# A transformer block in one kernel: the differences of w_down one section later and on GpSimd alone, x in pieces at block changes, the sums of a block split between GpSimd and VectorE

## The chip, the cores and the metric

The kernel runs on one core of one Trainium2 chip. The metric is device time in microseconds (us) of one execution; every comparison is made against the kernel before, run on the same chip. The engines are named as in the profile: PE (TensorE, matmuls; PEld is its weight load), ACT (ScalarE), DVE (VectorE), POOL (GpSimd) and SP (SyncE, which here does little but issue DMAs, in the order of its program).

## The reference

```python
def _A_ref(x, wqkv, wo):                 # 32 heads of 18
    qkv = (x @ wqkv).reshape(B, S, 3, H, Dh).transpose(2, 0, 3, 1, 4)
    q, k, v = qkv[0], qkv[1], qkv[2]
    p = softmax(einsum("bhqd,bhkd->bhqk", q, k) * (Dh ** -0.5), axis=-1)
    o = einsum("bhqk,bhkd->bhqd", p, v)
    return o.transpose(0, 2, 1, 3).reshape(B, S, D) @ wo

def _B_ref(x, w_gate, w_up, w_down):
    return (gelu(x @ w_gate) * (x @ w_up)) @ w_down

xn = layernorm(x)                        # x: 1 x 2048 x 576, fp32
out = x + _A_ref(xn, wqkv, wo) * silu(_B_ref(xn, w_gate, w_up, w_down))   # w_gate, w_up: 576 x 4608; w_down: 4608 x 576
```

## The kernel before, in words

All matmuls keep fp32 accuracy by splitting each operand into a high and a low part of a shorter type and adding three products (high·high, low·high, high·low). So every weight that comes from memory is cut in two on its way: `split` (L116 to L121) makes the high part with a `tensor_scalar` on POOL (L118) and the low part with a `tensor_tensor` on POOL (L120); `split_ap` (L123) makes the high part on ACT instead.

The feed-forward part sets the frame. The 2048 tokens are four blocks of 512 (`TB`). For each block the 4608 hidden columns are done in 18 rounds of two sections (`g` = 0 and 1); a section is one slice of 128 columns, so there are 144 sections, numbered `n`. A section does 27 pairs of matmuls `pg` and `pu` (gate and up, L534) in three chunks of 9. While it runs, the weights of the next section are asked for (`load_gu`, L132, the tile `raw`) and are cut in three pieces `wh`/`wl` (`split_gu`), one after each chunk. Then the hidden values are activated and cut into `ah`/`al`.

Sections 10 to 137 (`ATT`) also carry the attention in between the matmuls: score matmuls `pe` (L1027) that ACT turns into exponentials `pT` (L1028), and matmuls `pm` (L974) whose maxima DVE takes (L977). At the end of each section with `g` = 1 stand 64 matmuls with the values, `acc` (L1062), which ACT and DVE carry into `accs`. Sections 0 to 9 are a lead without it.

The down projection of a round follows one round later. In block 0 it is the plain product (`half_downs`, L602, 96 matmuls `py`). From round 18 on it is a scheme with seven products of half-sized matrices (`seven_downs`, L672), which needs sums and differences of the four quarters of w_down. These are made once, in block 0, by `cut_down`: it cuts the raw w_down of the round into `bh`/`bl` for block 0's own product, makes four differences of quarters in place in `raw` (POOL, L719), takes their high part into `TY` (ACT, L721) and their low part back into `raw` (POOL, L722), and stores quarters and differences with six DMAs into `ds[r]` (L724 to L726). Blocks 1 to 3 read `bh`/`bl` back from there (`load_seven`). The first five raw w_down sit in tiles of the attention (`pT`), the others in `raw`.

`raw` has two buffers for gate/up loads and w_down loads alike (`raw_wide`). The PE program is fixed by hand. The other engines' programs are ordered by a scheduler, save where an instruction is held in the order of the code (`kept`, `pin`). Each DMA on SP waits for its data or its buffer before the next one in SP's program is issued.

At a block change the transposed x of the next block is loaded by `load_xd`: six DMAs (`xd`, L155), each with a copy of the upper half of the partitions into the lower, three copies on POOL (L161) and three on ACT (L159). In the last round of a block, `add_copied` (L698, two additions) and `combine` (L704, seven additions and subtractions over `Y`) put the block's seven sums together, all on DVE, and `store_y` writes them. The change from block 0 to 1 has no combine, since block 0's down product is plain.

Of the kernel before, what the change touches and what calls it, by code (L numbers as in the profile page):

```python
# [17 lines left out]
P = 128  # L18
NT = S // P
TB = 512  # L20
# [59 lines left out]
def kernel(ctx: ExitStack, tc: tile.TileContext, x, wqkv, wo, w_gate, w_up, w_down, out):  # L80
# [67 lines left out]

    def load_xd(b, apart=False):

        xd, copies = [[], []], [[], []]
        for c in range(0, NC, XG):
            for i in range(2):
                t = wts.tile([P, XG, TB], F32R, name=f"xd{i}_{c}")
                asked[:] = [nc.sync.dma_start(f(t)[0:HR], xhs[b][i, c * HR:(c + XG) * HR, :]  # L155
                                              .rearrange("(k p) t -> p k t", p=HR))]
                xd[i].append(t)
                if apart and i:
                    copies[i].append(lambda t=t: nc.scalar.activation(t[HR:P], t[0:HR], AF.Copy))  # L159
                elif apart:  # L160
                    copies[i].append(lambda t=t: nc.gpsimd.tensor_copy(t[HR:P], t[0:HR]))  # L161
                else:
                    nc.gpsimd.tensor_copy(t[HR:P], t[0:HR])
        return (xd, copies) if apart else xd


# [3 lines left out]
    with tc.tile_pool(name="pro", bufs=1) as pro, tc.tile_pool(name="pps", bufs=1, space=PSUM) as pps:  # L170
# [286 lines left out]
        for b in range(NB):  # L457
# [37 lines left out]
    FF = {"w": ahead, "xd": XD, "down": [], "n": 0, "keep": None, "late": [], "marks": False, "between": [], "added": None,  # L495
          "after": []}
    AH, AL = (ffn.tile([P, 7, HALF], F32R, name=m) for m in ("ah", "al"))
# [165 lines left out]
    def seven_downs(b, r):  # L663
# [4 lines left out]
        for n, (p, t) in enumerate(SUMS):  # L668
# [13 lines left out]
            if done in (3, 4) and FF["between"]:  # L682
                keep(FF["between"].pop(0)())
        if not fresh:
            FF["after"].append(add_copied)
        if r == NR - 1 or b * NR + r == SEVEN.stop - 1:
            FF["after"].append(lambda: combine(b, r))

    def add_copied():

        places = [(SUMS[n][1], PRODUCTS[SUMS[n][0]][2]) for n in COPIED]
        for t in range(2):
            at_t = [i for i, (tt, _) in enumerate(places) if tt == t]
            for i in at_t:
                assert places[i][1] == places[at_t[0]][1] + at_t.index(i)
            yy = Y[:, t, places[at_t[0]][1]:places[at_t[-1]][1] + 1, :]
            low = TY[:, at_t[0]:at_t[-1] + 1:2, :]
            keep(nc.vector.tensor_tensor(yy, yy, low, op=ALU.add))  # L698

    def combine(b, r):  # L700

        for to, x, y, op in ((C11, C11, Q1, ALU.add), (Q1, Q1, Q6, ALU.add), (C22, C22, Q1, ALU.add), (C21, C22, C21, ALU.subtract),
                             (C22, C22, Q5, ALU.add), (Q1, Q1, Q5, ALU.add), (C12, C12, Q1, ALU.add)):
            keep(nc.vector.tensor_tensor(Y[:, :, to, :], Y[:, :, x, :], Y[:, :, y, :], op=op))  # L704
        if r == NR - 1:
            store_y(b, range(TB // P))

# [4 lines left out]

    def cut_down(r, raw, wd, keep=lambda i: i):

        raw = raw.rearrange("p g (c n) -> p (g c) n", c=2)
        b11, b12, b21, b22 = range(4)
        split(wd[0].rearrange("p g (c n) -> p (g c) n", c=2), wd[1].rearrange("p g (c n) -> p (g c) n", c=2), raw, keep)
        for to, x, y in ((b11, b12, b11), (b12, b22, b12), (b22, b22, b11), (b21, b22, b21)):
            keep(nc.gpsimd.tensor_tensor(raw[:, to], raw[:, x], raw[:, y], op=ALU.subtract))  # L719
        high, low = TY.bitcast(F32R), raw.bitcast(F32R)  # L720
        nc.scalar.activation(high, raw, AF.Copy)  # L721
        keep(nc.gpsimd.tensor_tensor(low, raw, f(high), op=ALU.subtract))  # L722
        for i, (four, t) in enumerate(((BH, high), (BL, low))):
# [50 lines left out]
    def section(specials=(), tag="f", raw_d=None, ahead=True):  # L774
# [16 lines left out]
        if n + 1 < NF:  # L791
            nxt = load_gu((n + 1) % (NR * G), keep) if ahead else FF.pop("next_gu")
        if g == G - 1 and seven(n):
            load_seven(r)
        elif g == G - 1:
            FF["rawd"] = FF.pop("first_d") if n < G else load_down(
                r, raw_d() if raw_d else raw_wide().rearrange("p (g n) -> p g n", g=G)) if ahead else FF.pop("next_d")

        def splits(k):
            if nxt and ahead:  # L800
                first = split_gu(nxt, k, pin)
                if k == 0 and n in ATT and n > ATT.start and not seven(n):
                    no_sync(first, FF["hl"], "hidden values first")

        for k in range(NG - 1):
# [5 lines left out]
        FF["w"] = nxt  # L811
        copies = [[], []]
        if n + 1 < NF and (n + 1) % (NR * G) == 0:
            FF["xd"], copies = load_xd(b + 1, True)
            for m in copies[0]:
                pin(m())
        FF["act"], FF["rest"] = activate(pg, pu, n < ATT.stop, pin, seven(n) and g == 0)
        now = FF["down"] and FF["down"][0][-1] < FF["n"]
        if n < ATT.stop and not now:
            run_rest()  # L820
        for m in copies[1]:
            pin(m())
        if g == G - 1:
# [13 lines left out]
    def finish(pool=ffn, cut=split):  # L837
# [12 lines left out]
        if n % G == G - 1:  # L850
            wd = [pool.tile([P, G, D], F32R, name=m) for m in ("dh", "dl")] if pool is not ffn and (n // G) % 2 else \
                [down_pair(BH), down_pair(BL)]
            if b == 0:
                cut_down(r, FF["rawd"], wd)
            else:
                cut(*wd, FF["rawd"])
            for h in range(2):
# [492 lines left out]
```

## Time and profile before

| what | value |
|---|---|
| median of 3 runs (2846.18, 2846.45, 3736.32) | 2846.45 us |
| the profiled execution's own time | 2844.66 us |
| its span, first to last instruction | 2842.9 us |
| PE busy | 2582.8 us (91%) |
| DVE busy | 2084.6 us (73%) |
| POOL busy | 1692.8 us (60%) |
| ACT busy | 1603.0 us (56%) |
| mean granted TensorE clock | 0.949 |

The third of the three runs lies far from the other two, so the median is the upper of two that agree. Busy shares are means over stages that differ: block 0 lasts until 1034 us, blocks 1 and 2 have their changes near 1600 and 2200 us, and the rest is the end. In the rows of a chain the columns are start (us), duration (us), engine, tile and line, with "x64" for so many in a row; "DMA raw<-in_B_w_down_dram" is a transfer from w_down into `raw`. In the rows of a table of windows they are the stretch, its length, then for each engine the busy time and the number of instructions, the granted clock, the DMA share and GB/s.

### The profile page before, as it was taken

How to read it: one execution, taken by the hardware profiler on the slowest of the kernel's cores; microseconds unless marked ns; L12 is line 12 of the kernel's file. 1: busy time of each engine (PE TensorE's matmuls, PEld its weight loads, DVE VectorE, ACT ScalarE, POOL GpSimd, SP SyncE). 2: the span in 40 equal slices, each digit the busy share in tenths (PEclk: the TensorE clock that was granted, in tenths of full speed). 3: DMA queues.
4: the chain of work that ended last, by engine and by line, in shares of the span. 5: the costliest groups of instructions: out<-in, count | busy, mean ns of one | idle time of the engine just before them, and what ended most of it. 6: DMA issues, size and time to landing. Idle time of an engine off the chain costs nothing.

```text
span 2842.9 us, 59879 instructions
## 1 busy us (share of the span) xinstructions
PE 2582.8 (91%) x21496; PEld 1957.3 (69%) x21496; DVE 2084.6 (73%) x3650; ACT 1603.0 (56%) x3022; POOL 1692.8 (60%) x2043
## 2 busy tenths in 40 slices
PE   9974477779778799999999899999999899999999
PEld 8863466566565577777776667677777577767788
DVE  5311356567566678899999789899999789989477
ACT  3211125556455476677676667667677567767622
POOL 3113355554555566776666666676676567677775
PEclk9996778889898899999999999999999899999999
DMA  8865345545556577676666766666666666666584
GB/s 258 271 221 168 138 159 152 158 138 148 148 150 162 148 191 201 180 184 176 184 187 177 190 184 179 176 173 180 180 187 192 165 180 194 182 182 176 151 219 142
DMA packets 438743, 506.96 MB, mean 178 GB/s; under 512 B 116096, under 2 KB 312736, under 8 KB 438160
## 3 DMA queue, kind: packets, MB, share of 16 engines
q1 hardware_dynamic: 438064, 488.97, 61.1%
q10 hardware_dynamic: 384, 14.16, 1.2%
q8 instruction: 173, 2.83, 0.4%
q14 instruction: 122, 1.00, 0.1%
HBM read 411.13 MB, written 106.02 MB: 182 GB/s over the span
## 4 chain that ended last, share of the span: by engine, by line
PE 78%; DMA 9%; POOL 5%; DVE 3%; issue 2%; ACT 2%; SPq 1%; ACTq 0%; POOLq 0%; DVEq 0%
PE pg L534 26%; PE acc L1062 15%; PE py L672 10%; PE pe L1027 8%; PE pm L974 8%; PE po L196 5%; PE py L602 3%; PE pu L534 2%; PE po L1210 2%; DMA raw<-in_B_w_up_dram 2%; POOL bl L120 1%; POOL raw L719 1%; DMA xd<-xhs 1%; DMA raw<-in_B_w_down_dram 1%; DVE mx L977 1%
## 5 line engine op out<-in xcount | busy, mean ns | idle before, releaser
L977 DVE TENSOR_REDUCE mx<-pm 128x1 f32<-128x512 f32 x2048 | 1267.7, 682 | 286.5 <-PE pm L974 268.1
L1028 ACT ACTIVATE pT<-pe 128x512 f32<-128x512 f32 x2048 | 1151.8, 598 | 453.8 <-PE pm L974 315.0
L534 PE MATMUL pg<-xd,wh 64*128 64x512 f32 x2592 | 956.2, 402 | 0.0
L534 PE MATMUL pu<-xd,wh 64*128 64x512 f32 x2592 | 955.8, 402 | 0.1
L1027 PE MATMUL pe<-q,Ks 64*128 64x512 f32 x2048 | 797.1, 397 | 115.6 <-ACT pT L1028 114.8
L974 PE MATMUL pm<-Km,q 64*128 64x512 f32 x2048 | 806.7, 399 | 31.5 <-ACT accs L1065 16.9
L534 PEld LDWEIGHTS pg<-xd,wh 64*128 64x128 f32 x2592 | 493.3, 190 | 142.8 <-POOL ah L118 37.7
L120 POOL TENSOR_TENSOR wl<-raw,wh 128x384 fp32r<-128x384 f32 x432 | 438.6, 1016 | 249.9 <-PE pu L534 223.2
L534 PE MATMUL pg<-xd,wl 64*128 64x512 f32 x1296 | 512.3, 395 | 14.0 <-POOL wl L120 14.0
L534 PE MATMUL pu<-xd,wl 64*128 64x512 f32 x1296 | 512.0, 395 | 0.0
L534 PEld LDWEIGHTS pu<-xd,wh 64*128 64x128 f32 x2592 | 493.8, 190 | 6.3 <-ACT vn L358 0.4
L1027 PEld LDWEIGHTS pe<-q,Ks 64*128 64x128 f32 x2048 | 380.0, 189 | 156.2 <-ACT pT L1028 121.2
L1062 PE MATMUL acc<-pT,VS 128*32 128x512 f32 x4096 | 454.2, 595 | 0.0
L974 PEld LDWEIGHTS pm<-Km,q 64*128 64x128 f32 x2048 | 385.6, 189 | 81.2 <-ACT accs L1065 17.8
L1062 PEld LDWEIGHTS acc<-pT,VS 128*32 128x32 f32 x4096 | 127.4, 110 | 291.4 <-issue 276.8
L118 POOL TENSOR_SCALAR wh<-raw 128x384 fp32r<-128x384 f32 x432 | 224.4, 520 | 148.3 <-DMA raw<-in_B_w_up_dram 79.6
L120 POOL TENSOR_TENSOR al<-t,ah 128x512 fp32r<-128x512 f32 x279 | 278.5, 998 | 23.2
L534 PEld LDWEIGHTS pg<-xd,wl 64*128 64x128 f32 x1296 | 245.6, 190 | 57.3 <-POOL wl L120 14.4
L534 PEld LDWEIGHTS pu<-xd,wl 64*128 64x128 f32 x1296 | 245.3, 189 | 2.8
L672 PE MATMUL py<-bh,ah 128*128 128x288 f32 x700 | 212.4, 303 | 0.6 <-DVE Y L680 0.5
L672 PE MATMUL py<-bl,ah 128*128 128x288 f32 x700 | 206.9, 296 | 0.0
L672 PE MATMUL py<-bh,al 128*128 128x288 f32 x700 | 205.5, 294 | 0.0
(196 smaller groups left out, 3731.3 us busy)
## 6 DMA issues: line engine op xcount, KB each, us to landing
Km<-kx SPq DMA_DIRECT2D x496, 108.0 KB
Ks<-kx SPq DMA_DIRECT2D x496, 108.0 KB
bh<-ds SPq DMA_DIRECT2D x50, 1008.0 KB
bl<-ds SPq DMA_DIRECT2D x50, 1008.0 KB
raw<-in_B_w_gate_dram SPq DMA_DIRECT2D x144, 288.0 KB
raw<-in_B_w_up_dram SPq DMA_DIRECT2D x144, 288.0 KB
VS<-vs SPq DMA_DIRECT2D x128, 152.0 KB
qk<-t SPq DMA_DIRECT2D x72, 256.0 KB
```

The costliest lines, as they stand in the source:

```text
L118: first = nc.gpsimd.tensor_scalar(hi, raw, 1.0, 1.0, op0=ALU.mult, op1=ALU.mult)
L120: low_part[:] = [keep(nc.gpsimd.tensor_tensor(lo, raw, f(hi), op=ALU.subtract))]
L196: nc.tensor.matmul(o, st, m, start=(i == 0), stop=(i == len(TERMS) - 1))
L534: nc.tensor.matmul(o, w[1 + wp][k][rr, c, :], xd[xp][k][rr, c, :], start=(i == 0), stop=(i == len(terms) - 1))
L602: return nc.tensor.matmul(py, hs[g][a][rr, j * P:(j + 1) * P], wd[w][rr, g, 288 * c:288 * c + 288], start=start, stop=stop)
L672: nc.tensor.matmul(py, x[:, a, t * P:(t + 1) * P], y[:, w, :], start=(i == 0), stop=(i == 2))
L974: nc.tensor.matmul(pm, QS[u, r][rr, t * P:(t + 1) * P], keys(KM, u, c, r)[rr, :], start=True, stop=True)
L977: return nc.vector.tensor_reduce(MX[u][:, 2 * r + a, t, c:c + 1], pm, axis=AX.X, op=ALU.max)
L1027: nc.tensor.matmul(pe, keys(KS, u, c, r)[rr, t * P:(t + 1) * P], QS[u, r][rr, :], start=True, stop=True)
L1028: nc.scalar.activation(PT[u, kt][:, 2 * r + a, :], pe, AF.Exp, scale=SCALE)
L1062: nc.tensor.matmul(ACC[u][32 * a:32 * a + 32, :], VS[(u * NA + c) % VB][:, v:v + 32], pt[:, a, :], start=first, stop=last, skip_group_chec ...
L1210: nc.tensor.matmul(po, parts_of(b, j)[x_][:, k, :], OW[w][c][k], start=(i == 0), stop=(i == len(OUT) - 1))
```

## The change

Three things are changed.

First, `cut_down` is taken apart. The plain cut into `bh`/`bl` stays where it was, at the end of the section with `g` = 1 (in the lead through `split_ap`, so with `bh` on ACT). The differences, `cut_differences`, are made one section later, behind the second piece of weights of the section with `g` = 0, and their high part `TY` is made by POOL as well (through `split`). The stores into `ds[r]` move with it.

Second, at a block change x is asked for in three pieces, at the three points at which weights are cut, and all six copies are POOL's.

Third, in the last rounds of blocks 1 and 2 and in the last seven-product round of all (round 67), `add_copied` and the first three steps of `combine` are made by POOL at the start of the next section with `g` = 1, and the other four steps by DVE at that section's end. `load_seven` is called later in the section.

```diff
-    def load_xd(b, apart=False):
+    def load_xd_part(b, xd, c, keep=lambda i: i):
+        for i in range(2):
+            t = wts.tile([P, XG, TB], F32R, name=f"xd{i}_{c}")
+            asked[:] = [nc.sync.dma_start(f(t)[0:HR], xhs[b][i, c * HR:(c + XG) * HR, :].rearrange("(k p) t -> p k t", p=HR))]
+            keep(nc.gpsimd.tensor_copy(t[HR:P], t[0:HR]))
+            xd[i].append(t)
...
+        last = r == NR - 1 or b * NR + r == SEVEN.stop - 1
         if not fresh:
-            FF["after"].append(add_copied)
-        if r == NR - 1 or b * NR + r == SEVEN.stop - 1:
-            FF["after"].append(lambda: combine(b, r))
+            FF["soon" if last else "after"].append(lambda: add_copied(nc.gpsimd if last else nc.vector))
+        if last:
+            FF["soon"].append(lambda: combine(nc.gpsimd, (C11, C11, Q1, ALU.add), (Q1, Q1, Q6, ALU.add), (C22, C22, Q1, ALU.add)))
+            FF["after"].append(lambda: combine(nc.vector, (C21, C22, C21, ALU.subtract), (C22, C22, Q5, ALU.add),
+                                               (Q1, Q1, Q5, ALU.add), (C12, C12, Q1, ALU.add)))
+            if r == NR - 1:
+                FF["after"].append(lambda: store_y(b, range(TB // P)))
...
-    def cut_down(r, raw, wd, keep=lambda i: i):
+    def cut_differences(r, raw):
         raw = raw.rearrange("p g (c n) -> p (g c) n", c=2)
         b11, b12, b21, b22 = range(4)
-        split(wd[0].rearrange("p g (c n) -> p (g c) n", c=2), wd[1].rearrange("p g (c n) -> p (g c) n", c=2), raw, keep)
         for to, x, y in ((b11, b12, b11), (b12, b22, b12), (b22, b22, b11), (b21, b22, b21)):
             keep(nc.gpsimd.tensor_tensor(raw[:, to], raw[:, x], raw[:, y], op=ALU.subtract))
         high, low = TY.bitcast(F32R), raw.bitcast(F32R)
-        nc.scalar.activation(high, raw, AF.Copy)
-        keep(nc.gpsimd.tensor_tensor(low, raw, f(high), op=ALU.subtract))
+        split(high, low, raw, keep)
...
-        if g == G - 1 and seven(n):
-            load_seven(r)
-        elif g == G - 1:
+        if g == G - 1 and not seven(n):
...
+            x_part(k)
+            if k == 1 and g == 0 and FF["later"]:
+                FF["later"].pop()()
+
+        new_x = n + 1 < NF and (n + 1) % (NR * G) == 0
+        xd = [[], []]
+        if g == G - 1:
+            while FF["soon"]:
+                FF["soon"].pop(0)()
+
+        def x_part(k):
+            if new_x:
+                load_xd_part(b + 1, xd, XG * k, tc.keep_in_program_order)
...
+        if new_x:
+            x_part(NG - 1)
+            FF["xd"] = xd
+        if g == G - 1 and seven(n):
+            load_seven(r)
         FF["act"], FF["rest"] = activate(pg, pu, n < ATT.stop, pin, seven(n) and g == 0)
...
-        for m in copies[1]:
-            pin(m())
...
+            cut(*wd, FF["rawd"])
             if b == 0:
-                cut_down(r, FF["rawd"], wd)
-            else:
-                cut(*wd, FF["rawd"])
+                FF["later"].append(lambda raw=FF["rawd"]: cut_differences(r, raw))
```

What the scheduler makes of it is seen best in one round of block 0 on POOL. Before, at the end of a section with `g` = 1, the cut of w_down into `bh`/`bl`, the four differences and their low part stand in one piece between two pieces of gate/up weights:

```order
L120 TENSOR_TENSOR al<-t_6840,ah 128x512
L118 TENSOR_SCALAR wh<-raw 128x384
L118 TENSOR_SCALAR bh<-raw 128x1152
L120 TENSOR_TENSOR bl<-raw,bh 128x1152
L719 TENSOR_TENSOR raw<-raw 128x288 x4
L722 TENSOR_TENSOR raw<-raw,TY 128x1152
L120 TENSOR_TENSOR wl<-raw,wh 128x384
```

In that form `TY`, which L722 reads, is made by ACT. Now, from the cut of one round's w_down (`bh`, `bl`) over the five operations on gate/up weights that follow it to the section after, the program of POOL around the differences is:

```order
L118 TENSOR_SCALAR wh<-raw 128x384
L120 TENSOR_TENSOR wl<-raw,wh 128x384
L118 TENSOR_SCALAR wh<-raw 128x384
L120 TENSOR_TENSOR wl<-raw,wh 128x384
L716 TENSOR_TENSOR raw<-raw 128x288
L118 TENSOR_SCALAR wh<-raw 128x384
L716 TENSOR_TENSOR raw<-raw 128x288 x3
L118 TENSOR_SCALAR TY<-raw 128x1152
L120 TENSOR_TENSOR raw<-raw,TY 128x1152
L120 TENSOR_TENSOR wl<-raw,wh 128x384
L118 TENSOR_SCALAR ah<-t_6840 128x512
L120 TENSOR_TENSOR al<-t_6840,ah 128x512
```

The differences have moved behind two pieces of the next section's weights, and `TY` stands among POOL's own instructions.

On ACT, in the same round, the high part stood among the exponentials; it has gone from ACT's program and nothing has come in its place:

```order
L607 ACTIVATE mark<-mark 128x1 x4
L1028 ACTIVATE pT<-pe 128x512 x3
L721 ACTIVATE TY<-raw 128x1152
L1028 ACTIVATE pT<-pe 128x512 x13
L549 ACTIVATE t_5428<-pg 128x512
```

On SP, in block 0, the stores into `ds` and the load of the next round's w_down stood a section apart before. The end of one round's stores and the gate/up loads behind them read:

```order
L724 DMA ds_124<-bl 128x288
L726 DMA ds_124<-TY 128x1152
L725 DMA ds_124<-bl 128x576
L726 DMA ds_124<-raw 128x1152
L924 DMA Ks<-kx_108 54x512 x2
L924 DMA Km<-kx_109 54x512 x2
L138 DMA raw<-in_B_w_gate_dram 64x9x128
L138 DMA raw<-in_B_w_up_dram 64x9x128
L862 DMA num<-oT 72x256
```

Now the last two stores come a section later, and the next round's w_down (L767) is asked for right behind them and one pair of gate/up loads:

```order
L722 DMA ds_123<-TY 128x1152
L722 DMA ds_123<-raw 128x1152
L928 DMA Ks<-kx_108 54x512 x2
L928 DMA Km<-kx_109 54x512 x2
L138 DMA raw<-in_B_w_gate_dram 64x9x128
L138 DMA raw<-in_B_w_up_dram 64x9x128
L767 DMA raw<-in_B_w_down_dram 128x2x576
L969 DMA q_7752<-zq 10x512
```

The w_down of a round goes into the buffer of `raw` that the store above it empties, and all gate/up loads of block 0 from there on share the other buffer.

37 lines of the change are left out of this document (10 added, 27 removed).

## The prediction

> **What bounds the kernel now.** I read the page first, then a table of windows, then the chain of waits inside single stages.
>
> ```profile
> PE 78%; DMA 9%; POOL 5%; DVE 3%; issue 2%; ACT 2%; SPq 1%; ACTq 0%; POOLq 0%; DVEq 0%
> ```
>
> Over the whole span the chain is matmuls for 78%. A faster helper engine can win only in the other 22%, so the question is where these lie. The windows below are cut at starts of the 64 `acc` matmuls, one group per round, so lengths divide into rounds: 1 round, 10, 1, 1 in block 0; 15 in block 1; and the changes from block 1 to 2 and 2 to 3.
>
> ```profile
> 459.85:515.74 55.89, 41.31 (x384) 31.35 (x388) 29.91 (x56) 25.55 (x52) 31.80 (x31) 0.85 0.41 123
> 515.74:949.05 433.31, 354.51 (x3324) 265.91 (x3328) 279.75 (x491) 236.69 (x456) 229.38 (x240) 0.89 0.55 154
> 949.05:1000.01 50.96, 35.52 (x337) 26.18 (x340) 28.02 (x49) 24.64 (x46) 24.66 (x26) 0.86 0.65 150
> 1000.01:1034.53 34.52, 34.52 (x336) 26.80 (x340) 27.48 (x50) 26.11 (x48) 18.27 (x23) 0.96 0.76 200
> 1067.26:1559.74 492.48, 492.48 (x4174) 358.63 (x4178) 442.69 (x781) 344.31 (x639) 334.35 (x433) 1.00 0.66 184
> 1559.74:1676.97 117.23, 103.25 (x839) 73.89 (x842) 97.43 (x163) 72.40 (x131) 76.06 (x94) 0.93 0.64 182
> 2169.31:2287.22 117.91, 104.67 (x838) 74.71 (x842) 98.59 (x162) 72.67 (x131) 75.82 (x93) 0.93 0.64 182
> ```
>
> In block 1 PE is busy all the time at a clock of 1.00, and a round takes 492.48/15 = 32.8 us. In block 0 ten rounds take 43.3 us each, with PE idle for 79 us of 433 and a clock of 0.89. The one round of block 0 without `cut_down`, the fourth row, has no idle PE and takes 34.5 us. So block 0 loses about 9 to 10 us in each of twelve rounds, and blocks 1 and 2 bind on PE except at their ends. The chain inside two rounds of block 0 says to what:
>
> ```profile
> 645.60 7.00 PE acc L1062 x64
> ...
> 658.50 0.22 PE pm L974
> ...
> 663.38 5.32 DMA raw<-in_B_w_down_dram
> 669.03 1.17 POOL bh L118
> 670.27 2.68 POOL bl L120
> 673.02 0.80 POOL raw L719
> ...
> 676.45 1.16 ACT TY L721
> 677.62 0.49 ACT pT L1028
> 678.15 0.79 PE pe L1027
> 678.95 0.85 PE pg L534 x2
> ...
> 682.25 0.23 PE pg L534
> ...
> 700.75 5.20 DMA num<-oT
> ...
> 708.55 0.74 POOL num L873
> ```
>
> ACT comes to `TY` in its program and waits there for four differences, which wait for `bl`, `bh` and the landing of w_down. Behind `TY` stand the exponentials `pT`, and PE waits for those before it may write the next scores. The stall also halves the clock: two matmuls take 0.85 us at 678.95, and one takes 0.23 again at 682.25, about 4 us after the start.
>
> **The change part by part.** *Block 0.* These rows are the instructions on `raw` in all stages (count, then shortest/median/longest in ns); the last row is from the answer on L719, what waited for the differences, us and times:
>
> ```profile
> L118 POOL TENSOR_SCALAR wh<-raw x432: 502/514/1023, 138.3 to 2795.0; 128x384 fp32r<-128x384 f32 x144
> L120 POOL TENSOR_TENSOR wl<-raw,wh x432: 992/1014/1400, 139.2 to 2795.6; 128x384 fp32r<-128x384 f32 x144
> L719 POOL TENSOR_TENSOR raw<-raw x52: 791/792/792, 477.0 to 986.7; 128x288 f32<-128x288 f32 x52
> L118 POOL TENSOR_SCALAR bh<-raw x14: 1152/1159/1169, 472.7 to 2698.1; 128x1152 fp32r<-128x1152 f32 x14
> L120 POOL TENSOR_TENSOR bl<-raw,bh x14: 2609/2620/2678, 474.3 to 2699.3; 128x1152 fp32r<-128x1152 f32 x14
> L722 POOL TENSOR_TENSOR raw<-raw,TY x13: 2642/2644/2644, 481.7 to 988.7; 128x1152 fp32r<-128x1152 f32 x13
>   ACT TY L721: 134.9, 17
> ```
>
> With `TY` off ACT, the wait in the last row (134.9 us over 17 rounds, the lead's among them) cannot occur, since nothing on ACT waits for w_down. What is late next? PE alone would need 33 us a round (34.52 at a clock of 0.96 is 33.1 at full clock). The other candidate is a new loop. In the changed order w_down(r+1) has the buffer that the last store of the differences of round r empties, and all gate/up loads share the other buffer, so each waits for the last `wl` of the one before. Both were spread over two buffers. A gate/up load that PE waited for shows what such a load costs:
>
> ```profile
> 529.91 6.56 DMA raw<-in_B_w_up_dram
> ```
>
> Once around, if nothing of it overlaps: the store, for which there is no row on the chain, between 0 and the 5.32 us of the w_down load, which moves as much (I take 4, since a load beside others is its nearest row); the w_down load 5.4; `bh` and `bl` 3.8; then `wl, wh, wl, wh, wl`, 3 x 1.01 + 2 x 0.51 = 4.1; only then the next gate/up load, 6; `wh, wl, wh, wl` 3.1; four differences with one `wh` among them, 4 x 0.79 + 0.51 = 3.7; `TY` 1.16 (POOL's `bh` has the same shape and 1.159) and the low part 2.64, 3.8. Together 4 + 5.4 + 3.8 + 4.1 + 6 + 3.1 + 3.7 + 3.8 = 33.9. Every second round has a `num` of 0.74 among them, and the K loads and gate/up issues stand ahead of w_down on SP: about 34.5. The loop is thus as long as PE's own round, and where two such chains are coupled each takes some of the other's jitter; I add 1.5 and take 36 us a round. POOL itself has room: 229.4 us in 433 now, which with 10 x 1.16 more is 241 in 360, or 67%.
>
> The first of the twelve rounds is 55.9 long, 12.6 above the ten; I leave half of that excess, 42. The last is 51.0, 7.7 above, with x of the next block in it; there POOL gets three copies more (1.46 each, a row below); I leave all of the excess, 44. So 10 x 36 + 42 + 44 = 446 against 55.89 + 433.31 + 50.96 = 540.2: **-94**. The round after them now carries the differences of the last w_down, 4 x 0.79 + 1.16 + 2.64 = 7 us on POOL with 16 us free; I take **+3** (0 to 7).
>
> *Block changes 1 to 2 and 2 to 3.* The last two windows hold three rounds each, 98.5 at 32.8; so the changes cost 18.7 and 19.4 us. The first of them has two parts (rows of the chain, then of ACT's, POOL's and DVE's timelines, the chain's end last):
>
> ```profile
> 1599.57 9.68 DMA Ks<-kx
> ...
> 1609.70 0.61 ACT accs L1065
> ...
> 1610.35 0.79 PE pm L974
> ```
>
> ```profile
> 1608.19 1.48 ACT L159 ACTIVATE xd<-xd 64x1536 fp32r<-64x1536 f32 x1 [4.13 <-DMA xd<-xhs]
> ```
>
> ```profile
> 1604.23 1.26 POOL L120 TENSOR_TENSOR al<-t,ah 128x512 fp32r<-128x512 f32 x1
> ...
> 1606.39 1.46 POOL L161 CAST xd<-xd 64x1536 fp32r<-64x1536 f32 x1 [0.90 <-DMA xd<-xhs]
> ...
> 1643.17 1.68 POOL L120 TENSOR_TENSOR al<-t,ah 128x512 fp32r<-128x512 f32 x1
> ```
>
> ```profile
> 1639.45 1.95 DVE L698 TENSOR_TENSOR Y<-Y,TY 128x576 f32<-128x576 f32 x2
> 1641.44 8.04 DVE L704 TENSOR_TENSOR Y<-Y 128x576 f32<-128x576 f32 x6
> ```
>
> ```profile
> 1651.82 0.79 PE pm L974
> ```
>
> ACT carries `accs` out only after the third copy of x, at 1609.70, and PE gets its bank at 1610.35. Without the copies on ACT this goes; but K landed at 1609.25 (1599.57 + 9.68), and in the new order the x and K loads stand on SP in the same sequence at these changes, pieces or not. What is late next is K, 0.4 us earlier. I take -1 (0 to -6: K's transfer took 9.68 beside those of x, and if the pieces thin these out it may take as little as the 5.20 of `num<-oT`).
>
> Later DVE holds PE up to 1651.82 with nine operations on `Y` of about 1.0 and 1.15 us (8.04/7 with one cut off by `accs`). Five of the nine go: 1.95 + 3 x 1.15 = 5.4 off DVE's chain. On POOL the five cost about 1.31 each (half of `bl`, which has twice the columns), 6.6, at the section's start, ahead of the `wh` and `wl` of that section, of which the first two can wait that long before PE needs them. DVE's other four need POOL's three; they come only at the section's end. I take **-5**. So -6 for each change, **-12** (0 to -22); and **-3** (0 to -5) for the same edit in the last seven-product round, where the output projection waits for `Y`.
>
> Two statements of the Trainium skill speak against this part. By "GPSIMD Engine Reference", section 3.1, an addition of two inputs takes GpSimd 1.96 times what VectorE takes; here the ratio of rows of like shape is 1.31/1.15 = 1.1, so the five would be 6.6 by the rows and 10 by the page, and the section's weights would come 3 us later than I count. By "SBUF — State Buffer", "Who interferes with whom", a VectorE instruction with two inputs in SBUF and a GpSimd instruction that reads it exclude each other for their whole length. The two `al` rows agree with interference, 1.26 us alone and 1.68 beside DVE's work on `Y`, but not with a full block each time; by the page's rule POOL's five would lose up to 5 x 1.15 more and the -5 would be about 0.
>
> *The lead.* Sections 0 to 9 change order: the loads of three sections' weights now stand ahead of the first stores of differences, ACT cuts `bh`, and the stores go later. The chain there goes through transfers, the largest being
>
> ```profile
> 325.88 26.36 DMA ds<-pT
> ```
>
> That store of differences would now be asked for elsewhere, and the gate/up loads with it. I cannot say which transfer is late next: **0**, from -25 to +25 (this one transfer gone, or another like it).
>
> Sum: -94 + 3 - 12 - 3 + 0 = -106. The profiled execution took 2844.66 (its span 2842.9 and 1.8 around it) and the median is 2846.45, 1.8 above it: 2846.45 - 106 = **2740 us**.
>
> **The rivals.** *A: the loop hides behind PE.* If the gate/up load after `wl` overlaps other steps, rounds go at PE's own 33.5: 10 x 33.5 + 36 + 38 = 409, -131 in place of -94, so 2703. For it: the 6 us load is counted in line with POOL although POOL has `ah`, `al` and idle time beside it. Against it: 33.9 was counted without any contention. *B: the two shared buffers bind.* If each round pays one more load of 6.56 that the two-buffer rotation hid, 34.5 + 6.6 = 41 a round: 10 x 41 + 46 + 49 = 505, -35 in place of -94; with the rest 2799, no difference by 2%. For it: the 5.20 us of `num<-oT` stand on the chain of the second round shown, so what stands in SP's line is not all hidden. *C, slower: SP's line.* The two stores now stand ahead of four K and Q loads, of gate/up and of w_down. If POOL reaches the differences late, since its pieces wait for PE to free `wh`, the stores wait, and everything behind them; PE waits for K, frees `wh` late, and the circle closes at the sum of both chains. It decides at a round of 45.0, the present mean (540.2/12); at 52 a round, which is the loop's 34.5 with PE's g = 0 section of about 17 (half of 34.52) in series, block 0 takes 624, +84, and with +3 - 12 - 3 the result is 2918. Against it: K has tiles to spare in block 1, whose queue is as full (DMA share 0.66 against 0.55). *D: x in pieces does nothing*, as SP's order at the changes says, and the DVE part is eaten by POOL: -12 becomes 0, 2752; that lies within the forecast's own range.
>
> **How the numbers follow.** Forecast (rounds of 34.5 to 39, the lead within ±25): 0.62, D in it, 2700 to 2785. A: 0.18. B: 0.15. C: 0.05. A measurement of this kernel can tell about 2% from no change, here below 2789.5 or above 2903.4. Faster: 0.62 + 0.18 + 0.03 of B with a lucky lead = 0.83; same: 0.12; slower: 0.05. The range goes from A with some of the lead's gain, 2685, to B, 2805.
>
> **What would show it.** On ACT no wait for a difference and no `TY`; rounds of block 0 at 36 us from `acc` to `acc`; where PE still stops, gate/up weights (`wh`, `wl`) as the releaser, behind a load into `raw`. A chain with `raw<-in_B_w_up_dram` in nearly every round and 41 us would show B; K tiles waiting behind `ds` stores, C. At the changes PE's first gap should end with K's landing, and DVE should have four operations on `Y` and let PE go about 5 us sooner. The forecast is wrong if block 0 wins less than 60 us, or if the lead moves by more than 25.

## The result and the profile after

The changed kernel takes 2819.49 us (median of 4 runs, 2817.7 to 2827.5) against 2846.45 for the kernel before on the same chip (median of the three of its four runs that agree; the fourth took 3736.32): a ratio of 0.9908, 95% interval 0.9883 to 0.9933. It is faster by 0.9%, about 26 us; 2740 was forecast, and 2685 to 2805 as the range. By the bound of 2% it makes no difference.

The windows of the changed kernel, cut at the starts of the 64 `acc` matmuls like those of before (the first round of block 0, ten, the last, the three rounds after them, 14 rounds of block 1, and the two later block changes):

```profile
463.50:500.40 36.90, 36.90 (x382) 30.50 (x380) 28.66 (x55) 23.92 (x50) 21.87 (x22) 1.00 0.52 147
500.40:918.10 417.70, 359.00 (x3321) 274.75 (x3320) 280.83 (x491) 228.06 (x446) 242.09 (x248) 0.93 0.58 154
918.10:959.20 41.10, 35.66 (x336) 26.75 (x334) 27.97 (x48) 22.51 (x46) 25.21 (x26) 0.92 0.62 167
959.20:1012.20 53.00, 38.88 (x338) 27.60 (x338) 27.78 (x51) 23.13 (x47) 33.34 (x32) 0.84 0.71 166
1012.20:1057.00 44.80, 34.81 (x281) 26.08 (x279) 27.69 (x49) 22.60 (x43) 26.17 (x38) 0.89 0.74 217
1057.00:1089.90 32.90, 32.90 (x280) 24.19 (x278) 27.72 (x53) 23.27 (x45) 21.36 (x29) 1.00 0.85 212
1089.90:1549.30 459.40, 459.40 (x3896) 334.50 (x3895) 415.05 (x729) 320.83 (x597) 314.77 (x408) 1.00 0.65 181
1549.30:1659.30 110.00, 103.23 (x836) 74.52 (x834) 91.45 (x157) 68.59 (x128) 84.31 (x100) 0.95 0.70 191
2151.70:2261.20 109.50, 103.28 (x840) 73.73 (x838) 94.36 (x157) 68.60 (x128) 83.78 (x98) 0.95 0.70 190
```

Set against the windows of before, stage by stage (us; the times of `acc` starts not quoted there are read from the same trace):

| stage | before | after | change | forecast |
|---|---|---|---|---|
| until the first `acc` (the lead) | 459.8 | 463.5 | +3.7 | 0 |
| block 0, first of twelve rounds | 55.9 | 36.9 | -19.0 | -14 |
| block 0, ten rounds | 433.3 | 417.7 | -15.6 | -73 |
| block 0, last round | 51.0 | 41.1 | -9.9 | -7 |
| the next three rounds (block 0 to 1) | 100.2 | 130.7 | +30.5 | +3 |
| change 1 to 2 (three rounds) | 117.2 | 110.0 | -7.2 | -6 |
| change 2 to 3 (three rounds) | 117.9 | 109.5 | -8.4 | -6 |
| all the rest | 1507.6 | 1507.2 | -0.4 | -3 |
| span | 2842.9 | 2816.6 | -26.3 | -106 |

Two rows hold the miss. The ten rounds of block 0 take 41.8 us each instead of 36, with PE idle for 59 us of 418, and at the change from block 0 to 1 some 27 us go that the forecast didn't have. The first of the two shows most clearly in one time around a round of block 0 in the chain of waits, from one request for w_down to the next:

```profile
711.41 7.71 DMA raw<-in_B_w_down_dram
719.27 1.15 POOL bh L118
720.50 2.63 POOL bl L120
723.13 0.95 POOL wl L120
724.64 1.01 POOL wl L120
726.22 1.02 POOL wl L120
728.38 8.17 DMA raw<-in_B_w_up_dram
...
737.32 1.34 POOL wl L120
739.22 1.02 POOL wl L120
...
744.12 1.17 POOL TY L118
745.36 2.68 POOL raw L120
748.06 3.67 DMA ds<-raw
751.80 7.30 DMA raw<-in_B_w_down_dram
```

No PE and no ACT stands in it: the chain runs from one w_down load to the next through GpSimd and three transfers, in 751.80 - 711.41 = 40.4 us. It is the loop that the prediction added up to 33.9, with longer loads. It is also the clearest of eleven such stretches, and the only one without PE. Of the ten from 496.03 to 918.05 us seven take 39.6 to 40.9 us, with 0 to 13 us of PE in the chain. The other three (from 576.91, 664.48 and 751.80) take 45.2 to 47.2, and in each of them the chain goes through 18 to 22 us of PE and then through `rb`, the reciprocal sums of the attention on their way back from memory. GpSimd's `num` waits for `rb`, and the differences stand behind `num`. The rows from the second of the three:

```profile
689.47 6.33 PE py L599 x96
...
697.01 4.23 DMA rb<-rT
701.37 0.74 POOL num L877
```

GpSimd's waits in the ten rounds agree. The largest of its waits with operations on `raw`, first before (window 515.74 to 949.05), then after (500.40 to 918.10; us in all, times, longest):

```profile
POOL wl L120 <- PE pu L534: 68.3, 37, 4.5
```

```profile
POOL wh L118 <- DMA raw<-in_B_w_up_dram: 104.3, 14, 8.3
```

The wait of `wh` was 20.7 us in 2 waits before, and that of `wl` for PE does not occur in these rounds any more: GpSimd used to wait for PE to free weights, and now waits for weights to land.

### The profile page after: what moved, and what is told of

The parts are those of the page before. It is cut to its first block, busy times and chain, and to the rows that moved or that the text cites. A ratio compares the mean times of both kernels' runs of the same rounds, so it can differ in the third digit from the quotient of the medians.

```text
span 2816.6 us, 59869 instructions
## 1 busy us (share of the span) xinstructions
PE 2586.9 (92%) x21496; PEld 1967.8 (70%) x21496; DVE 2074.6 (74%) x3635; ACT 1577.8 (56%) x2999; POOL 1739.7 (62%) x2081
## 4 chain that ended last, share of the span: by engine, by line
PE 73%; DMA 12%; POOL 9%; issue 2%; SPq 1%; DVE 1%; ACT 1%; POOLq 0%; ACTq 0%; DVEq 0%
PE pg L531 24%; PE acc L1066 12%; PE py L669 10%; PE pe L1031 7%; PE pm L978 7%; PE po L193 5%; PE pu L531 3%; DMA raw<-in_B_w_down_dram 3%; PE py L599 2%; POOL wl L120 2%; PE po L1214 2%; DMA raw<-in_B_w_up_dram 2%; DMA raw<-in_B_w_gate_dram 2%; POOL raw L716 1%; POOL raw L120 1%
## 5 line engine op out<-in xcount | busy, mean ns | idle before, releaser
L531 PE MATMUL pg<-xd,wh 64*128 64x512 f32 x2592 | 954.0, 401 | 10.9 <-DMA xd<-xhs 10.5
L531 PEld LDWEIGHTS pu<-xd,wh 64*128 64x128 f32 x2592 | 490.6, 189 | 31.6 <-POOL xd L154 22.6
```

The costliest lines, as they stand in the source:

```text
L531: nc.tensor.matmul(o, w[1 + wp][k][rr, c, :], xd[xp][k][rr, c, :], start=(i == 0), stop=(i == len(terms) - 1))
```

## The experiments

Times are medians, ratios are to the kernel before on the same chip with their 95% intervals, and "a round" is the mean of the 11 rounds from the first `acc` of block 0 on (44.5 us before, 41.3 after). Theory L is the loop through the two buffers of `raw`.

**A third buffer.** The raw w_down of block 0 goes into slots of `Y` that block 0 leaves free, so the two buffers of `raw` serve gate/up loads alone; the order on GpSimd stays. (Views of the tile that are reshaped to fit are left out of the cut.)

```diff
-                r, raw_d() if raw_d else raw_wide().rearrange("p (g n) -> p g n", g=G)) if ahead else FF.pop("next_d")
+                r, raw_d() if raw_d else Y[:, 0:2, 4:6, :] if b == 0
+                else raw_wide().rearrange("p (g n) -> p g n", g=G)) if ahead else FF.pop("next_d")
```

> The changed kernel, but the raw w_down of block 0 lies in four slots of Y that block 0 leaves free, so that gate/up loads have both buffers of raw to themselves. Theory L (the loop through the shared buffers sets the round: store of the differences, w_down load, bh and bl, three wl, gate/up load, differences): the gate/up load of 9.3 us leaves the loop, a round falls from 41.3 us to PE's 33 to 35, and the time from 2819 to about 2735 (2725 to 2750). Theory P (the order on GpSimd sets it, whatever the buffers): a round stays at 40 or more and the time at 2805 or more.

Measured: 2753.24 us, ratio 0.9686 (0.9666 to 0.9706); a round is 35.9 us. The ten rounds after the first (window from 496.42 to 854.58) leave PE idle for 15 us, not 59:

```profile
496.42:854.58 358.16, 342.86 (x3322) 263.07 (x3321) 288.79 (x491) 227.49 (x446) 247.48 (x250) 0.99 0.66 181
```

Theory P falls, since the differences stand behind the same two pieces of weights on GpSimd as in the changed kernel and the rounds are 5.4 us shorter. The time is 3 us beyond the range given for theory L, and the round 0.9 us above its 33 to 35.

**The engine alone.** The kernel before, with one edit: the high part `TY` is GpSimd's, the differences stay at their old place.

```diff
-        nc.scalar.activation(high, raw, AF.Copy)
-        keep(nc.gpsimd.tensor_tensor(low, raw, f(high), op=ALU.subtract))
+        split(high, low, raw, keep)
```

> The kernel before with one edit: the high part TY is made by GpSimd, the differences stay where they were. Theory L: ACT's wait is gone and no buffer is shared in a new way, so rounds of block 0 fall from 45 to 36 to 40 and the time to 2770 to 2800, below the changed kernel's 2819. Theory Q (GpSimd's block of bh, bl, differences, TY and low part, 12 us in one piece, takes ACT's place, since wl stands behind it): rounds stay at 44 to 46, the time at 2835 to 2860.

Measured: 2777.18 us, ratio 0.9765 (0.9747 to 0.9782); a round is 37.9 us, PE idle for 30 us of 379:

```profile
491.58:870.30 378.72, 349.13 (x3321) 269.41 (x3321) 286.25 (x491) 226.96 (x446) 250.79 (x253) 0.95 0.63 173
```

One line of the change gives 2.3% by itself, more than all of it together. In the chain of this kernel w_down lands in 4.8 us, not 7.7, and what follows it is GpSimd's block in one piece:

```profile
669.27 4.77 DMA raw<-in_B_w_down_dram
674.21 1.16 POOL bh L118
675.45 2.68 POOL bl L120
678.20 1.14 POOL raw L719
...
682.04 1.15 POOL TY L118
683.28 2.61 POOL raw L120
685.89 0.96 POOL wl L120
686.89 0.79 PE pg L534
```

So the new wait that theory Q described is there (PE starts when `wl` behind the block is done), but PE is idle for 3 us a round, where it was 8 before.

**The place alone.** The changed kernel with `TY` back on ACT.

```diff
-        split(high, low, raw, keep)
+        nc.scalar.activation(high, raw, AF.Copy)
+        keep(nc.gpsimd.tensor_tensor(low, raw, f(high), op=ALU.subtract))
```

> The changed kernel with TY back on ACT (the differences a section later, as in the changed kernel). Theory L: the loop holds the same terms, only 1.16 us of it on ACT, and ACT's wait is short because the differences' input has been there for long: 2815 to 2835. Theory E (what was won came from taking TY off ACT): ACT waits again for GpSimd in each round, 45 us or more, 2850 or more.

Measured: 2823.1 us, ratio 0.9928 (0.9908 to 0.9947); a round is 42.5 us. ACT still waits for the differences, now 82.2 us in 12 rounds,

```profile
ACT TY L718 <- POOL raw L716: 82.2, 12, 12.5
```

and yet the engine of `TY` is worth only 1.2 us a round. With the differences in the later place the loop binds, and who waits inside it matters little. With them in the old place the same edit of the engine gives 66 us. My expectation that ACT's wait would be short was wrong; it is hidden behind the loop. At the change from block 0 to 1 the engine counts for more: the four rounds from the last of block 0 on take 159.2 us in this run and 171.8 in the changed kernel, and the wait for q that is described below is not there. Why is open.

**The engine and the third buffer, the old place.** The kernel before with the edits of the first and the second experiment.

> The kernel before with TY on GpSimd, differences at their old place, and w_down in the free slots of Y in block 0. Theory L: with the differences at their old place the loads are not in one loop, and what is left of the stall there is GpSimd's block of 12 us ahead of wl; a third buffer gives little, 2765 to 2777, within 12 us of the run with the engine alone. Rival: w_down's late request, behind the release of a buffer, is most of what is left (rounds 37.9 to 34.5): 2735 to 2745.

Measured: 2748.09 us, ratio 0.9659 (0.9645 to 0.9674); a round is 35.8 us:

```profile
492.83:848.67 355.84, 341.19 (x3322) 264.34 (x3321) 280.22 (x491) 227.20 (x446) 250.29 (x255) 0.98 0.66 183
```

That is 29 us below the engine alone, not within the 12 that theory L allowed, and near the rival: the request for w_down waits for a buffer in the old order too. With a third buffer the place of the differences is worth nothing in these rounds (35.8 and 35.9).

**Sums as before.** The changed kernel with `add_copied` and all seven steps of `combine` on VectorE.

```diff
-            FF["soon" if last else "after"].append(lambda: add_copied(nc.gpsimd if last else nc.vector))
+            FF["after"].append(lambda: add_copied(nc.vector))
         if last:
-            FF["soon"].append(lambda: combine(nc.gpsimd, (C11, C11, Q1, ALU.add), (Q1, Q1, Q6, ALU.add), (C22, C22, Q1, ALU.add)))
-            FF["after"].append(lambda: combine(nc.vector, (C21, C22, C21, ALU.subtract), (C22, C22, Q5, ALU.add),
+            FF["after"].append(lambda: combine(nc.vector, (C11, C11, Q1, ALU.add), (Q1, Q1, Q6, ALU.add), (C22, C22, Q1, ALU.add), (C21, C22, C21, ALU.subtract), (C22, C22, Q5, ALU.add),
...
```

> The changed kernel with add_copied and combine on VectorE alone, as before. By the prediction each of the changes 1 to 2 and 2 to 3 is longer by 5 us, and nothing else moves: 2819 + 10 (+3 at the end) = 2829 to 2832. If x in pieces made the gain at the changes, the time stays within 3 us of 2819.

Measured: 2841.57 us, ratio 0.9989 (0.9975 to 1.0002). The changes 1 to 2 and 2 to 3 take 117.9 and 119.1 us instead of 110.0 and 109.5, which is 7.9 and 9.6 us and the whole gain there, more than the 5 expected; the end does not move (555.7 us after the last of these windows against 555.4). 3.9 us of the rest are in the lead, where this edit changes nothing, so they are scatter of the lead. In this run PE waits for VectorE, which comes to `accs` only behind its additions; in the changed kernel it does not:

```profile
1645.91 0.79 PE L977 MATMUL pm<-Km,q 64*128 64x512 f32 x1 [5.40 <-DVE accs L1070]
```

The rows of the changed kernel that answer to those of before, on DVE and on POOL:

```profile
1629.31 4.94 DVE L704 TENSOR_TENSOR Y<-Y 128x576 f32<-128x576 f32 x4
```

```profile
1617.76 2.83 POOL L700 TENSOR_TENSOR Y<-Y,TY 128x576 f32<-128x576 f32 x2
1620.66 4.45 POOL L704 TENSOR_TENSOR Y<-Y 128x576 f32<-128x576 f32 x3
```

DVE has 4.9 us there instead of 1.95 + 8.04 + 1.16, and POOL's five took 7.3 us, all of it 4 us before DVE's four start.

**x as before.** The changed kernel with `load_xd` of before: six loads at the section's end, three copies on GpSimd, three on ACT.

```diff
...
-            x_part(k)
...
-        if new_x:
-            x_part(NG - 1)
-            FF["xd"] = xd
+        copies = [[], []]
+        if new_x:
+            FF["xd"], copies = load_xd(b + 1, True)
+            for m in copies[0]:
+                pin(m())
...
+        for m in copies[1]:
+            pin(m())
```

> The changed kernel with x loaded as before: six loads at the section's end, three copies on GpSimd, three on ACT. Theory X (at the change from block 0 to 1, 40 us over the floor of four rounds instead of 19, the x copies on GpSimd between the cuts of weights are the cause): the four rounds from the last of block 0 on fall from 171.8 us to about 155 and the time to about 2803. Theory N (x is not the cause): they stay at 168 or more and the time within 5 us of 2819. For the changes 1 to 2 and 2 to 3 the prediction gave x 1 us each: they stay at 110 and 109.5 within 2 us; if x made the gain there, they go back to 115 to 118.

Measured: 2827.33 us, ratio 0.9935 (0.9913 to 0.9957), 8 us above the changed kernel where theory N allowed 5. The four rounds from the last of block 0 on take 174.7 us (65.9, 34.1, 41.7, 33.0), the changed kernel's 171.8: x moves the loss among the rounds, it does not make it. The later changes are 109.8 and 110.7, within 1.2 us of the changed kernel's. So x in pieces gives 1 us or nothing there, about as forecast, and theory X falls. With the third buffer as well, to see it without the loop:

> The changed kernel with both edits, the third buffer for w_down and x as before. If the two act apart: 2753 less what x as before gains or loses in the run with that edit alone. Theory X then expects about 2737, theory N 2753. If x's copies cost only because the loop keeps GpSimd late, the third buffer has taken that away and x as before gains nothing here.

Measured: 2760.24 us, ratio 0.969 (0.9663 to 0.9717), the four rounds 158.6 against 159.3 with the buffer alone. Again x makes no difference to their sum.

**The change from block 0 to 1.** In the changed kernel PE stands for 10 us twice here. The first time, in the round after block 0, it waits for a piece of x to land:

```profile
976.74 0.76 PE L531 MATMUL pg<-xd,wh 64*128 64x512 f32 x1 [10.47 <-DMA xd<-xhs]
```

With x as before PE stands for 22.6 us in the last round of block 0 instead, waiting for ACT's `pT`; the kernel before stands 12.9 us there. The second time, in the second round after block 0 (window from 1012.20), the chain is this, with SP's own line above it (`mT` carries the maxima of the scores through memory into a row of q, `rT` the reciprocal sums):

```profile
993.39 0.31 SPq L928 DMA_DIRECT2D Km<-kx  x1
1004.62 0.35 SPq L722 DMA_DIRECT2D ds<-TY  x1
1007.38 0.35 SPq L722 DMA_DIRECT2D ds<-raw  x1
...
1009.71 0.34 SPq L1004 DMA_DIRECT2D mT<-m2t  x1
```

```profile
1018.70 6.09 DMA rT<-sums
1024.86 0.65 SPq L867
1025.56 4.88 DMA q<-mT
1030.58 0.76 PE pe L1031
```

SP issues nothing for 11 us, because the next in its program is the store of `TY`, which GpSimd has not yet made; `mT`, `rT` and the q of the next attention stand behind it, and PE's next scores wait for q. Five runs went after this second stand. First, the last round's differences made at once instead of a section later:

```diff
-            if b == 0:
+            if b == 0 and r == NR - 1:
+                cut_differences(r, FF["rawd"])
+            elif b == 0:
                 FF["later"].append(lambda raw=FF["rawd"]: cut_differences(r, raw))
```

> The changed kernel, but the differences of the last round of block 0 (r = 17) are made at once as before, not a section later. Theory S (the 30 us lost at the change from block 0 to 1 come from SP standing at the last two stores, with mT, q and the K loads of the next attention behind them): most of the second stall, 12 us of it, goes, and the time falls from 2819 to 2800 to 2810. Theory X (they come from the x copies, now all on GpSimd between the weights): within 4 us of 2819.

Measured: 2822.0 us, ratio 0.9918 (0.9901 to 0.9936). The four rounds take 167.2 us instead of 171.8, far less than theory S gave, and the rounds before them 4 us more.

Second, the last round's two stores of differences issued by GpSimd, and third, those of all rounds of block 0 (the same line without its condition):

```diff
-            nc.sync.dma_start(ds[r][i, :, T1:T2 + 1, :], f(t))
+            (nc.gpsimd if r == NR - 1 else nc.sync).dma_start(ds[r][i, :, T1:T2 + 1, :], f(t))
```

> The changed kernel with one edit: the last round's two stores of differences (TY and low part, r = 17) are issued by GpSimd, behind its own instructions, instead of SP. Theory S (SP standing at these stores holds up mT, rT and q of the next attention): the third of the four rounds at the change from block 0 to 1 falls from 44.8 us to 33 to 35, the four from 171.8 to about 161, the time from 2819 to about 2808. Theory X2 (those transfers are late for another reason, PE and SP both being late from the round before): the third round stays at 42 or more.

> The same for all rounds of block 0. Theory C of the prediction (SP's line behind the stores sets the round): rounds fall from 41.3 us to 37 or less. Theory L (the buffers set it: w_down still waits for the store's landing and the gate/up loads still share a buffer): rounds stay at 39.5 to 42.5, and only the change to block 1 gains, as with the last round's stores alone.

Measured: 2819.74 us, ratio 0.9907 (0.9892 to 0.9922), and 2807.87, ratio 0.9867 (0.9848 to 0.9886). With the last stores alone the third of the four rounds still takes 40.5 us, and SP's line in that run says why:

```profile
1003.42 0.35 SPq L1004 DMA_DIRECT2D mT<-m2t  x1
1016.57 0.61 SPq L138 DMA_DIRECT2D raw<-in_B_w_gate_dram  x1
...
1019.20 0.66 SPq L1020 DMA_DIRECT2D q<-mT  x1
```

SP now stands 13 us at a gate load, whose buffer is freed by a `wl` that stands behind the same differences on GpSimd, and q is behind the gate load. With the stores of all rounds moved, a round is 40.9 us instead of 41.3 and the four at the change are 165.6 instead of 171.8: theory C of the prediction, SP's line as the bound of the rounds, is not what binds them. The third of these runs says something more. In it w_down is asked for 2.2 to 3.0 us behind the `up` load instead of 0.7 to 1.2, and it lands in 5.1 us instead of 7.7 (medians of ten rounds), while the store ahead of it takes 4.6 instead of 3.7. The seven shorter stretches from one request for w_down to the next fall from 40.4 to 39.6 us on average, and the three long ones stay at 45.2 to 46.3. So the length of the w_down load does not set the round by itself.

Fourth, both the third buffer and the moved stores:

> The changed kernel with the third buffer for w_down and the last round's two stores of differences issued by GpSimd. With the third buffer alone SP stood 9.5 us at the first of these stores, with the stores moved alone it stood 13 us at a gate load that waited for a shared buffer; either way q of the next attention came late. Theory S2 (SP's line is the cause and either standing point does it): with both gone the third of the four rounds at the change from block 0 to 1 falls from 43 to 45 us to 33 to 36, and the time from 2753 to about 2742 to 2745. If it stays at 40 or more, q is late for a reason that is not SP standing, and the cause stays open.

Measured: 2743.1 us, ratio 0.9649 (0.9628 to 0.9669). The third round is 35.6 us, as theory S2 has it, but the time of q hardly moved: the last three `q<-mT` are issued from 950.67 us on, with the buffer alone from 951.30 on, while the rounds ahead of them were 6 to 7 us later. SP stood 10 us at another gate load. Hence a last run, with the third buffer and the last differences at once:

> The changed kernel with the third buffer for w_down, and the differences of the last round of block 0 made at once. In the run with the buffer and the moved stores the third round at the change fell to 35.6 us, but only because the rounds before it were 6 us later; q of the next attention came at the same time, since SP still stood 10 us at a gate load whose buffer waits for a wl that stands behind the differences on GpSimd. Theory D (the place of the last round's differences, ahead of that wl, holds up SP whichever instruction it stands at): with them at once the third round falls to 33 to 34 us and the last four of the change from 159.3 to 148 to 153. If the third round stays above 36, the differences are not the cause, and x, which all these kernels but one have in common, is left.

Measured: 2743.49 us, ratio 0.9636 (0.962 to 0.9652); the third round 36.8 us, the four together 156.0 instead of 159.3 with the buffer alone. By what I had written a third round above 36 speaks against the differences as the cause, if only by 0.8 us, and the sum of the four is between the two theories. The longest wait of PE left here is again for a piece of x to land, 11.8 us, up to 916.60.

The four rounds of the changed kernel lie 20.6 us above those of before (171.8 and 151.2); the third buffer takes away 12.5 of that, the place of the last differences 3 to 5, with or without the buffer, and x as before none. The remaining 5 us are open, and so is how the 12.6 us that `TY` on ACT takes away fit in. The cause at this change is shown in part only.

**The best of the parts.** The kernel before with `TY` on GpSimd at the old place, the third buffer, and the sums split as in the changed kernel.

> The kernel before with three edits: TY on GpSimd with the differences at their old place, w_down in the free slots of Y in block 0, and the sums at a block's end split between GpSimd and VectorE as in the changed kernel; x as before. The parts add: 2748 less 8 at each of two changes and a few us in the lead gives 2728 to 2735. If the sums need the other moves beside them, 2745 or more.

Measured: 2735.82 us, ratio 0.9611 (0.9595 to 0.9628), 3% below the changed kernel. A round is 35.8 us, the changes 113.7 and 111.5 (121.0 and 116.5 in the run without the sums). The parts add within a microsecond of the range given.

## Why the prediction was wrong

**What bound the kernel before** was read rightly. Without ACT's wait, and nothing else changed, the kernel gains 2.3%. What it did not see is that the two buffers of `raw` hold up the old order too: the third buffer gave 29 us more there.

**The loop was named and its size missed.** Term by term, by the chain of the round from 711 us: the store 4 (3.67 measured), `bh` and `bl` with their gaps 3.8 (3.9), the three `wl` and two `wh` 4.1 (4.1), the next pieces 3.1 (2.9), the differences 3.7 (3.9), `TY` and the low part 3.8 (3.9). Those hold (the 2.9 leaves out the first `wh`, which is in the 2 us below). The step that failed is "the w_down load 5.4" and "the next gate/up load, 6": they took 7.7 and 8.2, and 2 us more passed until the gate/up load was issued and its first `wh` made. That is 6.4 of the 6.5 us between 33.9 and 40.4. The ten stretches from request to request took 422 us for the 360 forecast: 44 of the 62 missing are ten times 40.4 for 36, and the other 18 are the three long stretches, where a second step failed: `num` stood in the sum with its 0.74 us, and its wait for `rb` behind PE at nothing.

I had priced the loads from rows in which each was asked for alone or nearly so. In the new order SP asks for gate, up and w_down behind each other, as the order rows showed; in another round, SP's timeline has them so:

```profile
875.73 0.66 SPq L138 DMA_DIRECT2D raw<-in_B_w_gate_dram  x1
876.43 0.64 SPq L138 DMA_DIRECT2D raw<-in_B_w_up_dram  x1
877.35 0.41 SPq L767 DMA_DIRECT2D raw<-in_B_w_down_dram  x1
```

Three loads are asked for within 2 us, and the last takes 7.83 by the chain of waits. In the kernels where w_down is asked for by itself it lands in 4.7 to 5.6 us (medians of ten rounds). The run with the engine and the third buffer has both cases side by side: three of its ten w_down loads, asked for 0.7 us behind an `up` load, took 8.7 to 9.3 us, the other seven 3.9 to 6.9. That the loads share the queues' bandwidth is argued from this, not measured by itself. The `up` load of 8.2 us on the chain is another matter: no w_down is asked for beside it, but the stores of `bh` and `bl` and eight K loads are, in the 8 us ahead of it. What made it long was not tested.

Rival B had the figure, 41 a round, and I gave it 0.15. The mechanism it named, one more load of 6.56 per round that the rotation hid, is not what happened: no load was added to the loop, two that were in it grew, and in three rounds of ten another wait joined it. A mistake of judgment stands behind it. Where a sum of serial steps equals the other engine's round to a microsecond, an error in any term comes out in full on one side and hardly at all on the other; I took a value near the lower end and 1.5 for jitter.

**The change from block 0 to 1: +3 was wrong.** I counted 7 us of GpSimd for the moved differences of the last round and set them against GpSimd's 16 idle. That sum had no term for what waits behind this work: PE stood 10.0 us for q, ahead of which SP stood first at the moved stores and, with these gone, at a gate load behind the same GpSimd work. Nor had it one for x, whose piece PE waited 10.5 us for. The runs show the shares only in part (12.5 us by the third buffer, 3 to 5 by the place of the differences, the rest open). Rival C described SP's line, as a matter of every round; there, taking the stores off SP is worth 0.4 us a round.

**Block changes 1 to 2 and 2 to 3: right in the total**, -7.2 and -8.4 for -6 each, and the sums are the cause. The working was off in three places. The sums gave 7.9 and 9.6 for the 5 forecast. The part given to ACT's copies (-1) was 0 to 1, and PE's first wait does not end with K, as it should have, but with GpSimd's copies of x (3.85 us of waiting, up to 1601.57). And 8.04 us were divided by seven where the row counts six ("x6"): 1.34 us each. That is moreover VectorE's time beside a busy GpSimd, as these rows for the same operation show (shortest/median/longest in ns; VectorE from before, GpSimd from after):

```profile
L704 DVE TENSOR_TENSOR Y<-Y x21: 757/1165/1736, 1641.4 to 2718.7; 128x576 f32<-128x576 f32 x21
L704 POOL TENSOR_TENSOR Y<-Y x9: 1424/1434/1437, 1620.7 to 2678.0; 128x576 f32<-128x576 f32 x9
```

The two additions of VectorE at which GpSimd stood still (at 2713.40 and 2714.20 in the kernel before) took 0.76 us. GpSimd's took 1.42 to 1.44 us for the 1.31 forecast, so the ratio of the two undisturbed is 1.9, and the 1.96 that the Trainium skill states in "GPSIMD Engine Reference", section 3.1, agrees with it. The prediction's 1.1 was not a ratio of the engines. In the changed kernel GpSimd's five stand 4 us clear of VectorE's four, so the exclusion that the Trainium skill states in "SBUF — State Buffer", "Who interferes with whom", did not act between the two; VectorE's four still took 1.05 to 1.45 us each, beside other work of GpSimd.

**The end: 0 for -3**; DVE's work there hides behind something else, which no run looked into. **The lead** moved by +3.7 within the ±25, and by as much between kernels that are alike in it.

The range, 2685 to 2805, failed because the case that came, B plus a loss at the change, was priced at 2799 with its other terms taken as in the forecast; with the 27 us of the change on top, a range that held B would have reached 2827.

## What to carry to other kernels

When an operation is moved to free an engine, list the buffers that its operands hold until then and what is asked for behind them. Here one more section of lifetime for w_down turned two rotating buffers into two fixed ones and put two loads in a loop, while room for a third lay unused in another tile. A change made of several parts is worth taking apart: one line gave 2.3%, the sums 0.6%, x nothing, and the place of the differences took most of it back.

When a loop and the other engine's round come out equal, price the loop's transfers by what is asked for beside them in the new order, not by the old order's rows. And read an engine's time for an operation from a row in which the engine beside it stood still, or say that it didn't.

## What had not been expected of the hardware

A load of w_down (the same bytes each time) takes 4.7 us when asked for by itself, 5.3 in the order of before, 5.1 with the `up` load asked for 2.2 to 3.0 us ahead, and 7.7 when two gate/up loads are asked for within the 2 us ahead of it (medians of ten rounds of block 0). And the same two-input addition of 128 x 576 took VectorE 0.76 us while GpSimd stood still and 0.97 to 1.74 us while it worked throughout; on GpSimd it took 1.42 to 1.44 us, beside VectorE's maxima (one input) as well as beside nothing.
